# A gated FFT-filter and feed-forward kernel: x and part of w1 loaded first, the gate moved to VectorE and GpSimd, w2 moved to SyncE's queue, and the scheduler's transfer rates reset

## The chip, the cores and the metric

The kernel runs on one core of one Trainium2 chip. The time is device microseconds (us) of one execution. Each quoted time is a median of several fast executions. An execution counts as slow when it is over 1.5% above the fastest of the same kernel. "Span" is the length of the one profiled execution, from its first to its last instruction; it is about 2 us shorter than the time of that execution.

## The reference

```python
B, S, D, F = 1, 2048, 512, 1792              # x: (1, 2048, 512), bfloat16
g = sigmoid((x * gate_w).sum(-1, keepdims=True))
a = irfft2(rfft2(x) * (w_r + 1j * w_i))      # over (S, D)
h = x @ w1 + b1                              # (S, F)
b = (h * tanh(softplus(h))) @ w2             # Mish, then (S, D)
out = g * a + (1 - g) * b
```

Two independent paths read x, and the gate g joins them at the very end. TensorE does the Fourier transforms as matrix products. Two transposes between the stages go through scratch in device memory ("scr" in the profile).

## The kernel before

x is taken in 16 tiles of 128 rows. All work is declared as tasks with reads, writes and a priority. When the kernel is built, a list scheduler inside it gives each engine a fixed order of its tasks. It does this with its own guesses of how long everything takes. On the chip every engine goes through its list in order. When the head of the list isn't ready, the engine waits, even if later items could run.

```python
SYNC_LAT = 0.12
DMA_BW = 370e3        # bytes per us that the scheduler assumes for a transfer
XBAR_BW = 95e3
W_BW = 150e3          # ... for the reversed loads of w_r, w_i
NEARLY = 12           # tiles whose feed-forward result is parked before the last stage
# priorities: the ready task with the highest one goes first
PR = dict(ld=100.0, tr=99.5, a1=98.0, s1=99.0, mid=96.0, fin=94.0, mm1=80.0,
          act=90.0, mm2=70.0, out=95.0, gate=99.8, cp=95.5)
# ... in schedule(), for each task taken:
            free[t.eng] = est + t.dur
            if t.isdma:
                xs = max(est + t.dur + 1.2, bw_free)
                bw_free = xs + t.xfer          # t.xfer = bytes / bw
                t.done = bw_free + 0.9
            else:
                t.done = est + t.dur
            order[t.eng].append(t)
```

The five stages of TensorE work, under the names used below:

- **First stage**: FFT along D and part of S, 16 tiles. Its result is written to scratch and read back transposed.
- **Middle stage**: the rest of the FFT along S, the multiplication by w (on VectorE) and the first inverse step, 16 pairs; then scratch again.
- **Last stage**: the remaining inverse steps, then the mixing with g on VectorE.
- **First product**: x @ w1, 224 matmuls of 512 columns (after Mish on ScalarE, its result feeds the next).
- **Second product**: the Mish result @ w2, another 224 matmuls' worth.

The two products depend on the FFT nowhere. They are the *filler* that the scheduler puts into TensorE's list wherever it thinks that the FFT will not be ready. The second product can fill only once w2 has landed.

```python
        # loads, in order of issue on SyncE's queue (SP)
        ld_x(0, 1)
        ld_c(0, 0, 1280, ["FD", ("FT", 0)])    # FFT tables
        ld_x(1, 4)
        ld_w1(0)                               # first half of w1
        ld_c(1, 1280, 2816, [("FT", 1)])
        ld_x(4, 8)
        ld_w1(1)
        # ... rest of x, w_r, w_i, then:
        for o, W in (("Wa", Wa), ("Wb", Wb)):  # copy to the other half of the partitions
            for h in range(2):
                # ...
                G.add(f"cp{o}{h}", [("dve", ..., lambda e, ...: e.tensor_scalar(
                    out=W[64:128, js, :], in0=W[0:64, js, :], scalar1=sc, ...))],
                      reads=[(o, i) for i in range(4)], writes=[(o, 4, h)], prio=PR["cp"])
        # ... t_r1w: the four writes of the first stage's result to scratch
        for h in range(2):                     # w2 on GpSimd's queue, behind those writes
            dma(f"ld_w2_{h}", w2_sb[:, 7*h:7*(h+1), :], w2v[:, 7*h:7*(h+1), :], 128 * 7 * 1024,
                writes=[("w2", h)], deps=t_r1w, queue="pool")
        # ... the first product reads w1 in halves (ft // 7):
        G.add(f"mm1_{c}_{ft}", ..., reads=[...] + [("w1", ft // 7)], ..., prio=PR["mm1"] - 3 * c)
        # ... second product:
        G.add(f"mm2_{t}_{part}_{n0}", ..., prio=PR["mm2"] - 6 * c - 0.01 * n0)

        # the gate: 64 one-column matmuls, Tanh on ScalarE after all Mish, then the columns
        def f_gate(e):
            for t in range(NT):
                for dt_ in range(4):
                    ins = e.matmul(ps[:, bk(sl_g), t:t + 1], xT[:, dt_, t, :],
                                   gw_sb[:, dt_:dt_ + 1], start=(dt_ == 0), stop=(dt_ == 3))
            return ins
        G.add("gate", ..., deps=t_hs[-2:-1], prio=PR["gate"])
        G.add("gth", [("act", 1.6, lambda e: e.activation(gth[:, :], ps[:, bk(sl_g), 0:NT],
              AF.Tanh, scale=0.5))], reads=[sl_g], writes=["gth"], deps=t_hs, prio=PR["gate"])
        # gcol = 0.5 * gth + 0.5, omg = 0.5 - 0.5 * gth, ngcol = -gcol   (VectorE)
```

## Time and profile before

| before | |
|---|---|
| time, median of 3 runs | 146.09 us (145.66 to 146.83) |
| span of the profiled run | 142.7 us |
| TensorE busy | 134.9 us, 95% |
| first product starts | 9.86 us |
| first middle-stage matmul | 42.05 us |
| gate columns start on VectorE | 99.00 us |

The page of the profile gives busy time by engine, then each engine's busy tenths in 40 equal slices (9 is 90% or more), the granted clock and the DMA engines in the same slices, and shares of the chain of waits that ended last. PE is TensorE, DVE VectorE, ACT ScalarE, POOL GpSimd, SP SyncE. Lines of the page of the kernel before:

```profile
span 142.7 us, 2376 instructions
...
PE 134.9 (95%) x866; PEld 72.9 (51%) x881; DVE 86.1 (60%) x188; ACT 82.9 (58%) x139; POOL 3.9 (3%) x10
...
PE   6999999778979999999999999999999999999992
...
DMA  4999999999299999580303695000012120100121
...
PE 70%; DVE 13%; DMA 7%; ACT 4%; issue 3%; DVEq 0%; SPq 0%
```

TensorE is the limit: 95% busy, and most of the chain. The only slices below 9 between the first and the last are 8, 9, 10 and 12, which lie between about 25 and 43 us. The view of waits, for TensorE alone, says for what it stood (line waiting, what ended the wait, us in total, times, the longest):

```profile
PE ps L666 <- DVE R L515: 1.5, 2, 0.8
PE ps L530 <- DVE GD L527: 1.3, 1, 1.3
PE ps L748 <- DMA R<-scr: 0.8, 1, 0.8
PE ps L703 <- ACT hsb L812: 0.5, 1, 0.5
PE ps L824 <- DMA w_sb<-in_B_w_dram: 0.2, 1, 0.2
```

An eviction is the copy of a TensorE result out of PSUM, the memory that matmuls write to; VectorE does it as a CAST, ScalarE as an ACTIVATE. L666 is the first stage, L748 the first middle-stage matmul, L703 a small table step, L824 the second product, and L530 the warm-up at the start. The timeline lists start, duration, engine, line, operation, count, and in brackets the idle time before and what ended it. These lines of the kernel before (of several engines) show the two waits on VectorE, the wait for scratch, and the gate:

```profile
25.09 1.23 DVE L583 TENSOR_SCALAR Wa<-Wa 64x4112 bf16<-64x4112 bf16 x1 [1.94 <-DMA Wa<-in_A_w_r_dram]
...
26.34 1.29 DVE L515 CAST R<-ps 128x512 bf16<-128x512 f32 x2
...
27.09 0.28 PE L666 MATMUL ps<-CF,R 128*128 128x256 bf16 x1 [0.78 <-DVE R L515]
...
42.05 0.28 PE L748 MATMUL ps<-R,SM 128*128 128x256 bf16 x1 [0.76 <-DMA R<-scr]
...
95.64 1.74 PE L845 MATMUL ps<-gw_sb,xT 128*128 128x1 bf16 x64
...
97.49 1.28 ACT L849 ACT_TABLE_LOAD   x1 [2.47 <-PE ps L845]
...
99.00 0.17 DVE L852 TENSOR_SCALAR gcol<-gth 128x16 f32<-128x16 f32 x1 [12.28 <-ACT gth L849]
```

The first-stage matmul at 27.09 needs an eviction (CAST) that stood in VectorE's list behind a 1.23 us copy of Wa. The gate's 64 matmuls take 1.74 us, counted until the last result is out; then come a table load, Tanh and the column arithmetic. The Trainium skill, "ScalarE: Activation LUTs", section "What ACT_TABLE_LOAD costs", states about 1283 ns for such a load; the trace's 1.28 us agrees.

### The profile page before, as it was taken

The page shows a single profiled execution, that of the slowest core. Times are in us where ns is not written, and L with a number is a line of the kernel's source. Part 1 is how long each engine was busy: PE and PEld are TensorE (multiplying, and loading weights), DVE is VectorE, ACT ScalarE, POOL GpSimd, SP SyncE. Part 2 cuts the span into 40 slices and gives each one's busy share as a digit, 9 for nine tenths or more (in the row PEclk, how much of TensorE's full clock was granted, in tenths as well). Part 3 has the DMA queues.
Part 4 walks back from the last instruction along what each step waited for, and adds up shares of the span by engine and source line. Part 5 has one row for each costly group of instructions (what it writes and reads, how often), then busy time and mean ns, then how long its engine had stood idle before and what let it go on. Part 6 is the DMA issues. An engine that isn't in the chain of part 4 may idle for free.

```text
span 142.7 us, 2376 instructions
## 1 busy us (share of the span) xinstructions
PE 134.9 (95%) x866; PEld 72.9 (51%) x881; DVE 86.1 (60%) x188; ACT 82.9 (58%) x139; POOL 3.9 (3%) x10
## 2 busy tenths in 40 slices
PE   6999999778979999999999999999999999999992
PEld 2476665554434444434444465455456565555471
DVE  2448694974009999999971031002999985899331
ACT  3289888776867877779984573855154344431000
POOL 1000000000160000000000000000000000000000
PEclk9999999999999999999999999999999999999999
DMA  4999999999299999580303695000012120100121
GB/s 117 302 405 408 249 172 151 150 307 336 74 310 359 364 317 145 131 283 0 147 0 152 174 292 121 0 0 5 0 74 76 74 76 5 74 0 36 43 108 39
DMA packets 20463, 21.66 MB, mean 152 GB/s; under 512 B 5156, under 2 KB 16932, under 8 KB 20388
## 3 DMA queue, kind: packets, MB, share of 16 engines
q1 hardware_dynamic: 19712, 18.89, 49.6%
q0 software_dynamic: 704, 2.62, 5.2%
q8 instruction: 7, 0.11, 0.3%
q14 instruction: 4, 0.03, 0.1%
q10 hardware_dynamic: 36, 0.00, 0.0%
HBM read 14.17 MB, written 6.29 MB: 143 GB/s over the span
## 4 chain that ended last, share of the span: by engine, by line
PE 70%; DVE 13%; DMA 7%; ACT 4%; issue 3%; DVEq 0%; SPq 0%
PE ps L824 28%; PE ps L804 21%; PE ps L885 5%; PE ps L530 4%; DMA scr<-R 4%; DVE PX L764 3%; DVE PX L760 3%; DVE PX L763 3%; DMA R<-scr 3%; PE ps L866 3%; PE ps L654 2%; ACT R L516 2%; DVE PX L767 2%; DVE R L515 1%; PE ps L779 1%
## 5 line engine op out<-in xcount | busy, mean ns | idle before, releaser
L824 PE MATMUL ps<-w_sb,hsb 128*128 128x512 bf16 (+1 forms) x232 | 51.3, 366 | 0.6 <-DMA w_sb<-in_B_w_dram 0.2
L804 PE MATMUL ps<-xT,w_sb 128*128 128x512 bf16 x215 | 51.3, 379 | 0.4
L812 ACT ACTIVATE hsb<-ps,b1f 128x512 bf16<-128x512 f32 x56 | 37.7, 689 | 11.1 <-PE ps L804 10.8
L516 ACT ACTIVATE R<-ps 128x512 bf16<-128x512 f32 (+1 forms) x43 | 24.7, 596 | 16.3 <-PE ps L824 11.2
L824 PEld LDWEIGHTS ps<-w_sb,hsb 128*128 128x128 bf16 x238 | 22.7, 98 | 22.4 <-DMA w_sb<-in_B_w_dram 0.5
L804 PEld LDWEIGHTS ps<-xT,w_sb 128*128 128x128 bf16 x224 | 21.2, 98 | 22.9 <-ACT xT L621 0.2
L516 ACT ACTIVATE PX<-ps 128x512 bf16<-128x512 f32 (+1 forms) x19 | 10.5, 551 | 6.8 <-PE ps L885 4.2
L515 DVE CAST R<-ps 128x512 bf16<-128x512 f32 (+1 forms) x17 | 11.3, 689 | 3.3 <-PE ps L654 1.6
L876 ACT ACTIVATE TT<-ps 128x512 bf16<-128x512 f32 x11 | 6.4, 595 | 6.5 <-PE ps L866 6.4
L897 DVE SCALAR_TENSOR_TENSOR PX<-ps,gcol,R 128x512 f32<-128x512 f32 x12 | 9.0, 751 | 1.4 <-DVE R L891 0.5
L873 DVE CAST TT<-ps 128x512 bf16<-128x512 f32 x5 | 3.4, 689 | 9.7 <-PE ps L866 8.9
L885 PE MATMUL ps<-GD,TT 128*128 128x256 bf16 x64 | 9.0, 273 | 0.0
L530 PE MATMUL ps<-GD 128*128 128x512 bf16 x18 | 7.3, 522 | 1.3 <-DVE GD L527 1.3
L885 PEld LDWEIGHTS ps<-GD,TT 128*128 128x128 bf16 x64 | 6.2, 98 | 3.3 <-DVE TT L873 0.3
L852 DVE TENSOR_SCALAR gcol<-gth 128x16 f32<-128x16 f32 x1 | 0.2, 174 | 12.3 <-ACT gth L849 12.3
L767 DVE TENSOR_TENSOR PX<-PX 128x512 bf16<-128x512 bf16 x16 | 6.8, 425 | 1.0
L763 DVE TENSOR_TENSOR PX<-PX,Wb 64x512 bf16<-64x512 bf16 x16 | 6.8, 422 | 0.5
L764 DVE TENSOR_TENSOR PX<-PX,Wb 64x512 bf16<-64x512 bf16 x16 | 6.7, 421 | 0.2
L760 DVE TENSOR_TENSOR PX<-PX,Wa 128x512 bf16<-128x512 bf16 x16 | 6.7, 421 | 0.1
L923 DVE SCALAR_TENSOR_TENSOR R<-ps,omg,R 128x512 bf16<-128x512 f32 (+1 forms) x5 | 3.2, 643 | 5.8 <-PE ps L824 5.8
L903 DVE SCALAR_TENSOR_TENSOR R<-ps,gcol,PX 128x256 bf16<-128x256 f32 x12 | 5.8, 484 | 0.4
L654 PEld LDWEIGHTS ps<-CF,R 128*128 128x128 bf16 x64 | 4.7, 101 | 2.6 <-issue 0.6
(93 smaller groups left out, 110.9 us busy)
## 6 DMA issues: line engine op xcount, KB each, us to landing
scr<-R SPq DMA_DIRECT2D x8, 512.0 KB, 4.6
R<-scr SPq DMA_DIRECT2D x8, 512.0 KB, 6.0
w_sb<-in_B_w_dram SPq DMA_DIRECT2D x2, 896.0 KB, 8.8
w_sb<-in_B_w_dram POOLq DMA_DIRECT2D x2, 896.0 KB, 11.4
out_dram<-R SPq DMA_DIRECT2D x7, 256.0 KB, 2.0
R<-in_A_x_dram SPq DMA_DIRECT2D x3, 512.0 KB, 11.3
SM<-c_sm SPq DMA_DIRECT2D x1, 576.0 KB, 10.9
Wa<-in_A_w_r_dram SPq DMA_DIRECT2D x1, 514.0 KB, 13.9
```

The costliest lines, as they stand in the source:

```text
L515: G.add(name, [("dve", dve_dur(n), lambda e: e.tensor_copy(out=outf(), in_=inf())), ("act", act_dur(n), lambda e: e.activation(outf(), inf ...
L516: ("act", act_dur(n), lambda e: e.activation(outf(), inf(), AF.Copy))],
L530: G.add(f"warm{i}", [("pe", 0.43 if i < 7 else 0.22, lambda e, sl=sl: e.matmul(ps[:, bk(sl), :], GDf[:, 0:128], GDf[:, 0:512], start=True, ...
L760: return e.tensor_tensor(out=v(P1, sP, 0, 128), in0=v(Xb, sX, 0, 128), in1=Wa[:, js, 0:256], op=ALU.mult)
L763: e.tensor_tensor(out=v(P2, sQ, 0, 64), in0=v(Xb, sX, 64, 128), in1=Wb[64:128, js, 0:256], op=ALU.mult)
L764: return e.tensor_tensor(out=v(P2, sQ, 64, 128), in0=v(Xb, sX, 0, 64), in1=Wb[0:64, js, 0:256], op=ALU.mult)
L767: return e.tensor_tensor(out=P1[:, sP.i, :], in0=P1[:, sP.i, :], in1=P2[:, sQ.i, :], op=ALU.add)
L804: ins = e.matmul(ps[:, bk(sl), :], w1_sb[:, dt_, 128 * ft:128 * (ft + 1)], xT[:, dt_, 4 * c:4 * c + 4, :], start=(dt_ == 0), stop=(dt_ == 3))
L812: return e.activation(hsb[:, hb, ft, :], ps[:, bk(sl), :], AF.Mish, bias=b1f[:, ft:ft + 1])
L824: ins = e.matmul(ps[:, bk(sl), 0:n1 - n0], hsb[:, hb, ft, 128 * tl:128 * (tl + 1)], w2_sb[:, ft, n0:n1], start=(ft == 0), stop=(ft == NFT ...
L885: ins = e.matmul(ps[:, bk(sy), 256 * hh:256 * (hh + 1)], TT[:, st.i, i, :], GD[:, i, :], start=(i % 2 == 0), stop=(i % 2 == 1))
L897: return e.scalar_tensor_tensor(out=o, in0=ps[:, bk(sy), 0:256].unsqueeze(1).to_broadcast([128, 2, 256]), scalar=gcol[:, t:t + 1], in1=ya[ ...
```

## The change

The intent: let TensorE start real work earlier, give it more filler while the first scratch round trip is under way (so w2 has to be there earlier), and take the gate off TensorE and ScalarE, where it sits between the products and the last stage.

The diff, cut to its core:

```diff
-NEARLY = 12
+NEARLY = 8
-DMA_BW = 370e3
+DMA_BW = 380e3
-W_BW = 150e3
+W_BW = 130e3
 # (and given rates at single transfers: scratch writes 330e3 and 300e3, scratch reads
 #  300e3 and 296e3, the straight part of w_r, w_i 188e3, first x tiles 600e3 and 270e3)

 # start
-        ld_x(0, 1)
-        ld_c(0, 0, 1280, ...)
-        ld_x(1, 4)
-        ld_w1(0)                                  # half of w1
+        ld_x(0, 1, bw=600e3)
+        ld_x(1, 4, bw=270e3)
+        ld_w1(0)                                  # 512 of its 1792 columns
+        ld_c(0, 0, 1280, ...)
+        ld_w1(1)

 # w2
-        for h in range(2):
-            dma(f"ld_w2_{h}", ..., deps=t_r1w, queue="pool")
-        dma("ld_gd", ..., deps=t_r1w, queue="pool")          # inverse tables
-        dma("ld_gt", ..., deps=t_s1 + t_r1w, queue="pool")
+        ld_w2(0)                  # on SyncE's queue, right behind w_r, w_i and SM (middle-stage tables)
+        ld_w2(1, t_e2)            # t_e2: the evictions of the first stage
+        dma("ld_gd", ..., deps=t_e2)
+        dma("ld_gt", ..., deps=t_s1 + t_r1r)                 # t_r1r: the scratch reads

 # copies of Wa, Wb
-                      reads=[(o, i) for i in range(4)], writes=[(o, 4, h)], prio=PR["cp"])
+                      reads=[(o, i) for i in range(4)], writes=[(o, 4, h)], deps=t_e2, prio=PR["cp"])

 # second product
-    prio=PR["mm2"] - 6 * c - 0.01 * n0
+    prio=(76.0, 75.0, 58.0, 52.0)[c] - 0.01 * n0

 # gate
-        G.add("gate", 64 matmuls ...); G.add("gth", Tanh on ScalarE ...)
+        for h in range(4):
+            dma(f"ld_xg{h}", xg[:, 4*h:4*h+4, :], xv[:, 4*h:4*h+4, :], 128 * 4096, ...)  # x again
+            for t in range(4 * h, 4 * h + 4):
+                G.add(f"gx{t}", [("dve", 0.8, lambda e, t=t: e.scalar_tensor_tensor(
+                    out=xg[:, t, :], in0=xg[:, t, :], scalar=1.0, in1=gwb[:, :],
+                    op0=ALU.mult, op1=ALU.mult, accum_out=gacc[:, t:t + 1]))], ...)
+        # z = clip(gacc, -80, 80); ez = e ** z by GpSimd pow; omg = 1 / (1 + ez); gcol = ez * omg
```

There is also a rewrite of how the late tiles of the last stage are mixed, which goes with NEARLY = 8: the gate scale is applied on the way out of PSUM instead of in a separate step. Some small priorities and the scheduler's guess for the warm-up matmuls change too. The rates are used nowhere but in the scheduler. They transfer nothing faster; they only change what it believes, and so its order.

## The prediction

> **What bounds the kernel now.** TensorE: the page has it busy 95% of 142.7 us, 70% of the chain of waits; the stretch table shows granted clock 1.00. In the chain a 512-column matmul takes 0.216 us back to back. By counts: the feed-forward products 448 x 0.216 = 96.7; FFT first stage 8.9, middle 6.9, inverse 10.6; transposes 1.8; gate 1.6: about 126.5 us. The other 16.2 (stretches, timeline): start 7.2 (warm-up matmuls, waiting for x and w1); two late warm-ups 0.4; idle between 12 and 140 us 3.9; tail 2.5; 2.2 unassigned. Stalls (waits): 0.78 and 0.75 at 26.3 and 28.9 us (waiting for an eviction behind a 1.23 us copy of Wa on VectorE); 0.46 at 33.9 (table step); 0.76 at 42.0 (scratch read); 0.25 at 51.8 (w2).
>
> **What the change does.**
> 1. Gate off TensorE: 64 one-column matmuls, 1.58 us at 95.8, on the chain: saved. The Tanh table load (1.28 us at 97.5) goes too, off the path; the Trainium skill, "ScalarE: Activation LUTs", "What ACT_TABLE_LOAD costs", has 1283 ns; the trace agrees. The 16 new VectorE multiply-accumulates, 0.65 us each (estimate from the 0.64 us scalar-tensor-tensor), 10.4 us, fit VectorE's idle 76 to 97 us. GpSimd pow: no duration to go by.
> 2. Wa/Wb copies moved behind all evictions: the two 0.75 us stalls go (-1.5).
> 3. More fill: 112 first-product and 14 second-product matmuls stand ahead of the first middle matmul, against 88. Scratch, table and w2 stalls go (-1.4).
> 4. x, then 512 KB of w1, then tables: first product at about 7.8 instead of 9.9 us, no warm-up afterwards: -0.7.
> 5. DMA runs full from 4 to 36 us; w2's first half and the broadcast gate add 1.0 MB ahead of the scratch writes, 3 us at the trace's 340 GB/s, so scratch reads land at 44 to 48 instead of 42 us; the fill hides it. The Trainium skill, "DMA: Bandwidth & Descriptors", "Issuing engines are not separate DMA queues", has all issuers share 16 engines: w2 on SP gains only by starting earlier, into the 36 to 40 us gap (DMA 0.34 busy).
> 6. Given back: in the middle stage the filler is 7 matmuls per pair (1.94 us with the FFT's two) instead of 8 (2.16), while VectorE needs about 2.0: it becomes the limit, +1.5. The stage runs 47 to 79 us, not 42 to 75.
> 7. Late-tile rewrite (8 early tiles, not 12): VectorE 29 us against 35 us of TensorE work in the last stage; off the path.
>
> Sum: -1.6 -1.5 -1.4 -0.7 -0.4 (small) +1.5 = -4.1 if the middle loses in full, about -6 if not; I take -5.3.
>
> **Predicted: 140.8 us, 8 in 10 within 138.8 to 143.3.** Faster by over 2%: 0.87; within 2%: 0.11; slower: 0.02.
>
> **What would show it right:** no gate matmuls or second table load late; no waits over 0.5 us of first-stage matmuls on VectorE; first middle matmul at 46 to 49 us; VectorE over 95% busy in the middle stage with TensorE at 92 to 97%; gate columns ready before the chain needs them. **Wrong:** TensorE waiting on w2's second half or scratch reads near 44 to 48 us.
>
> **What would make it wrong.** w2's second half and inverse tables queue ahead of the scratch reads and stall the middle stage by several us; the second x load delays the second scratch round trip; pow takes over 6 us; the first w1 part lands after 8 us.

## The result, and the profile after

| | before | after |
|---|---|---|
| time, median (fast runs, same rounds) | 145.88 us (4 runs, 144.66 to 146.83) | 139.32 us (4 runs, 138.44 to 139.75) |
| ratio | | 0.957, 95% interval 0.9485 to 0.9655 |
| span | 142.7 us | 136.6 us |
| TensorE busy | 134.9 us, 95% | 131.3 us, 96% |
| VectorE busy | 86.1 us, 60% | 94.1 us, 69% |
| first product starts | 9.86 us | 7.76 us |
| first middle-stage matmul | 42.05 us | 45.40 us |
| 512-column feed-forward matmuls listed ahead of it | 88 | 126 (112 + 14) |

A ratio is the mean time of one kernel's fast runs over that of the other's of the same rounds, so it isn't quite the ratio of the quoted medians. The counts in the last row are read from the instruction order of the built kernels, not from the trace, which lacks some matmul records. In a pair such as 112 + 14, the first number is of the first product, the second of the second.

The page of the kernel after:

```profile
span 136.6 us, 2281 instructions
...
PE 131.3 (96%) x803; PEld 70.6 (52%) x817; DVE 94.1 (69%) x213; ACT 82.4 (60%) x137; POOL 3.6 (3%) x8
...
PE   6999999999999999999999999999999999999992
...
DMA  4999999999999923658853535990002101222021
...
PE 77%; DVE 17%; issue 4%; DVEq 0%
```

TensorE has no slice below 9 between the first and the last, and DMA is gone from the chain. TensorE's waits in the kernel after, all of them:

```profile
PE ps L537 <- DVE GD L534: 1.2, 1, 1.2
PE ps L783 <- DVE PX L771: 0.3, 1, 0.3
PE ps L816 <- issue: 0.2, 1, 0.2
```

Only the wait at the start is left, with two small ones (L783 is the inverse step of the middle stage). Its timeline around the scratch read and around the gate (the lines are of several engines and not adjacent):

```profile
42.38 3.19 PE L836 MATMUL ps<-w_sb,hsb 128*128 128x512 bf16 x14
45.40 0.27 PE L752 MATMUL ps<-R,SM 128*128 128x256 bf16 x1
...
77.42 0.68 DVE L802 SCALAR_TENSOR_TENSOR R<-R,gwb 128x512 bf16<-128x512 bf16 x1
...
95.78 2.91 POOL L856 TENSOR_TENSOR gz<-eul,gz 128x16 f32<-128x16 f32 x1 [94.37 <-DVE gz L855]
...
99.22 0.17 DVE L859 TENSOR_TENSOR gcol<-gz,omg 128x16 f32<-128x16 f32 x1
...
101.08 0.47 DVE L909 SCALAR_TENSOR_TENSOR R<-ps,ngcol,PX 128x256 bf16<-128x256 f32 x1
...
101.71 0.39 PE L871 MATMUL ps<-CF,R 128*128 128x128 bf16 x4
```

Fourteen second-product matmuls run up to the first middle-stage matmul, which has no idle time in front of it. They can only be there because w2's first half has landed. At the gate, VectorE gets the last quarter of the second load of x at 92.85 us; pow then takes 2.91 us on GpSimd while TensorE goes on with the first product. VectorE finishes the first tile of the last stage at 101.55 (101.08 + 0.47), and TensorE's next last-stage matmuls follow at 101.71. So the gate delays nothing, but at its end there is only about 0.15 us to spare.

**Where the 6.1 us of span went**, divided at the first middle-stage matmul. In the kernel after it starts 3.35 us later (45.40 against 42.05), but 38 more feed-forward matmuls of 0.216 us are done by then, 8.2 us of work: 4.9 us are won ahead of this point. From there to the end it takes 91.2 us against 100.65, 9.45 us less, for 9.8 us less work (the 8.2 and the gate's 1.6). So the gate's 1.6 us are won and about 0.35 us given back: 4.9 + 1.6 - 0.35 is the 6.1.

### The profile page after: what moved, and what is told of

Read it like the earlier page. It is cut to its first block, busy times and chain, and to the rows that moved or that the text cites. A ratio compares the mean times of both kernels' runs of the same rounds, so it can differ in the third digit from the quotient of the medians.

```text
span 136.6 us, 2281 instructions
## 1 busy us (share of the span) xinstructions
PE 131.3 (96%) x803; PEld 70.6 (52%) x817; DVE 94.1 (69%) x213; ACT 82.4 (60%) x137; POOL 3.6 (3%) x8
## 4 chain that ended last, share of the span: by engine, by line
PE 77%; DVE 17%; issue 4%; DVEq 0%
PE ps L816 35%; PE ps L836 21%; PE ps L890 5%; PE ps L537 4%; DVE PX L768 4%; DVE PX L767 4%; DVE PX L764 4%; DVE PX L771 3%; PE ps L652 3%; PE ps L871 3%; PE ps L610 1%; PE ps L664 1%; PE ps L665 1%; DVE R L518 1%; PE ps L783 1%
## 5 line engine op out<-in xcount | busy, mean ns | idle before, releaser
L816 PE MATMUL ps<-xT,w_sb 128*128 128x512 bf16 x216 | 49.7, 379 | 0.6 <-issue 0.2
L519 ACT ACTIVATE R<-ps 128x512 bf16<-128x512 f32 (+1 forms) x37 | 20.9, 596 | 8.1 <-PE ps L836 4.1
L518 DVE CAST R<-ps 128x512 bf16<-128x512 f32 (+1 forms) x19 | 12.7, 689 | 5.5 <-PE ps L652 3.8
L519 ACT ACTIVATE PX<-ps 128x512 bf16<-128x512 f32 x15 | 8.9, 597 | 5.8 <-DVE PX L764 2.2
L802 DVE SCALAR_TENSOR_TENSOR R<-R,gwb 128x512 bf16<-128x512 bf16 x16 | 10.0, 688 | 1.1 <-DMA R<-in_A_x_dram 1.1
L927 DVE SCALAR_TENSOR_TENSOR R<-ps,omg,R 128x512 bf16<-128x512 f32 (+1 forms) x9 | 6.2, 692 | 5.9 <-PE ps L836 5.7
L914 ACT ACTIVATE PX<-ps,gcol 128x256 f32<-128x256 f32 x8 | 3.7, 473 | 6.9 <-PE ps L890 6.9
L537 PE MATMUL ps<-GD 128*128 128x512 bf16 x18 | 6.0, 475 | 1.2 <-DVE GD L534 1.2
L902 DVE SCALAR_TENSOR_TENSOR PX<-ps,gcol,R 128x512 f32<-128x512 f32 x8 | 6.0, 752 | 0.7
L783 PE MATMUL ps<-PX,SM 128*128 128x512 bf16 x15 | 5.7, 381 | 0.4 <-DVE PX L771 0.3
## 6 DMA issues: line engine op xcount, KB each, us to landing
w_sb<-in_B_w_dram SPq DMA_DIRECT2D x2, 896.0 KB, 10.7
```

Of the source, the lines that this page charges most:

```text
L518: t = G.add(name, [("dve", dve_dur(n), lambda e: e.tensor_copy(out=outf(), in_=inf())), ("act", act_dur(n), lambda e: e.activation(outf(), ...
L519: ("act", act_dur(n), lambda e: e.activation(outf(), inf(), AF.Copy))],
L537: G.add(f"warm{i}", [("pe", 0.42 if i < 5 else 0.22, lambda e, sl=sl: e.matmul(ps[:, bk(sl), :], GDf[:, 0:128], GDf[:, 0:512], start=True, ...
L802: G.add(f"gx{t}", [("dve", 0.8, lambda e, t=t: e.scalar_tensor_tensor(out=xg[:, t, :], in0=xg[:, t, :], scalar=1.0, in1=gwb[:, :], op0=ALU ...
L816: ins = e.matmul(ps[:, bk(sl), :], w1_sb[:, dt_, 128 * ft:128 * (ft + 1)], xT[:, dt_, 4 * c:4 * c + 4, :], start=(dt_ == 0), stop=(dt_ == 3))
```

## The experiments

Two readings of that division compete.

- **The ledger**, on which the prediction was built: each part removes its own stall or work, and the parts add up.
- **The order**: what counts is whether the scheduler's fixed list has the right amount of filler at each point where the FFT depends on something slow. Then a part has no worth of its own. It may even cost, because it moves the list.

All twelve runs gave correct results and were timed in five rounds. "Ratio" is to the kernel before, which ran in the same rounds (medians 144.74, 144.85 and 144.88 us in the three groups); brackets are the 95% interval. Line numbers differ a little from kernel to kernel. Where the granted clock was below 1.00 for a while, this is said.

### Group 1: the kernel after, and one part of it undone

**after_again**: the kernel after, unedited.

> The changed kernel once more, as the yardstick for the runs beside it. All theories: ratio to before about 0.957 (0.950 to 0.963), profiled span 136.5 to 138, TensorE idle after 12 us about 1.5 us in sum.

Ratio 0.9592 [0.9559, 0.9625], median 138.87 us, span 136.9 us. The result repeats, on another set of rounds and with a narrower interval.

**a_gate_on_tensor**: the gate goes back to TensorE and ScalarE; the second load of x, the broadcast gate weights and pow go out.

```diff
-        for h in range(4): dma(f"ld_xg{h}", ...); 16 multiply-accumulates on VectorE; pow ...
+        G.add("gate", [("pe", 64 * 0.03, f_gate)], ..., deps=t_hs[-2:-1], prio=PR["gate"])
+        G.add("gth", [("act", 1.6, ... AF.Tanh ...)], ..., deps=t_hs, prio=PR["gate"])
```

> The changed kernel with the old gate: 64 one-column matmuls, Tanh on ScalarE, no second x load, no pow. Ledger theory (only TensorE time counts): 1.6 us slower than the changed kernel, ratio about 0.968, the 64 matmuls on the chain for 1.6 us and no other new TensorE wait above 0.5 us. Rival 1 (the gain is the latency of the gate: VectorE's 12 us wait and the late start of the last stage): 3 us or more slower, ratio 0.978 or above, with TensorE waiting in the last stage. Rival 2 (the gain is the order of the loads): unchanged or faster, ratio 0.957 or below, for 2 MB less is loaded.

Ratio 0.9908 [0.988, 0.9937], median 143.52 us, span 141.3 us. That is 4.65 us over after_again, for matmuls that take 1.6. The timeline shows the other three:

```profile
103.73 1.74 PE L851 MATMUL ps<-gw_sb,xT 128*128 128x1 bf16 x64
...
105.34 6.20 PE L830 MATMUL ps<-w_sb,hsb 128*128 128x512 bf16 x28
...
107.09 0.17 DVE L858 TENSOR_SCALAR gcol<-gth 128x16 f32<-128x16 f32 x1 [14.87 <-ACT gth L855]
...
111.38 0.39 PE L872 MATMUL ps<-CF,R 128*128 128x128 bf16 x4
```

And from its view of waits:

```profile
PE ps L891 <- ACT TT L882: 1.5, 2, 0.8
```

Tanh is put after all Mish, and so after the whole first product. In this order the first product runs until 102.4 us, against 94.3 in the kernel before, so the gate's columns come at 107.09 instead of 99.00. TensorE spends 28 second-product matmuls, 6.2 us, on covering the wait. These are then missing as filler between the last-stage tiles, and TensorE waits there twice for ScalarE (1.5 us) and runs at the pace of VectorE, which mixes one tile in about 2 us (the gate-scaled steps start at 107.76, 109.79 and 111.81). In sum TensorE is busy 2.3 us longer than in after_again (134.9 against 132.6) and waits 2.0 us longer (3.5 against 1.5), which is nearly the whole difference of the spans, 4.4. The gate's position is worth more than its duration. Of the readings, this fits Rival 1; b_gate_off_tensor below shows that an earlier gate alone brings nothing in the kernel before.

**a_copies_early**: the copies of Wa and Wb are no longer held back.

```diff
-                      ..., writes=[(o, 4, h)], deps=t_e2, prio=PR["cp"])
+                      ..., writes=[(o, 4, h)], prio=PR["cp"])
```

> The changed kernel with the Wa/Wb copies no longer held behind the last first-stage eviction. The scheduler reorders the FFT matmuls a little around them. Ledger theory: TensorE waits of 0.5 us or more on evictions come back near 25 to 31 us, 0.7 to 1.5 us in sum, ratio about 0.964. Rivals 1 and 2: no change, 0.957.

Ratio 0.9605 [0.9574, 0.9636], median 139.12 us: 0.25 us over after_again, with overlapping intervals. The copies are back between the evictions, at 25.61 and 28.19 us on VectorE, much as in the kernel before, and yet TensorE has no wait on an eviction. All its waits:

```profile
PE ps L537 <- DVE GD L534: 1.2, 1, 1.2
PE ps L783 <- DVE PX L771: 0.3, 1, 0.3
```

The list has four first-product matmuls between the first-stage tiles there, which cover it. So the two waits of 0.75 us in the kernel before came from the copies together with an order that had nothing to put in front of them.

**a_w2_gpsimd**: w2 and the inverse tables go back to GpSimd's queue, behind the scratch writes.

```diff
-        ld_w2(0)
-        ld_w2(1, t_e2)
+        ld_w2(0, t_r1w)                    # with queue="pool" inside ld_w2
+        ld_w2(1, t_r1w)
-        dma("ld_gd", ..., deps=t_e2)
+        dma("ld_gd", ..., deps=t_r1w, queue="pool")        # and ld_gt likewise
```

> The changed kernel with both halves of w2 and both inverse tables on the GpSimd queue behind the scratch writes, as before. By the instruction order the 14 second-product matmuls ahead of the middle stage are then gone, and 112 first-product ones remain. Ledger theory: scratch reads land earlier (42 to 43 us), so the lost filler costs only a short wait there plus waits for w2 at 44 to 52 us: 0.3 to 1.5 us slower, ratio 0.959 to 0.967. Rival 2: at least 3 us slower, 0.978 or above. Rival 1: no change.

Ratio 1.0172 [1.0138, 1.0207], median 147.4 us: 8.5 us over after_again, slower than the kernel before. One line of the timeline matters most:

```profile
49.82 3.17 PE L836 MATMUL ps<-w_sb,hsb 128*128 128x512 bf16 x7 [5.10 <-DMA w_sb<-in_B_w_dram]
```

TensorE came to the second product before w2 was there and waited 5.1 us. The wait itself had a price: seven matmuls took 3.17 us instead of the 1.67 that seven take elsewhere, because the granted clock had dropped to 0.50. It was half from about 48.2 to 55.0 us, so it had fallen while TensorE was still waiting.

### Group 2: the kernel before, with one part of the change alone

**b_gate_off_tensor**: the new gate, with its loads and pow.

```diff
-        G.add("gate", 64 matmuls ...); G.add("gth", Tanh ...)
+        (second load of x, 16 multiply-accumulates, pow, columns, as in the change)
```

> The kernel before with the new gate alone (VectorE products from a second x load, pow on GpSimd, no Tanh). Undoing it cost the changed kernel 4.6 us where the ledger had 1.6, so two readings are open. Ledger: 1.6 us faster than before, ratio 0.989. Coupled reading (the late gate also forces second-product matmuls, which are filler, to be spent ahead of the last stage, and there TensorE then waits for VectorE): in the kernel before, whose first-product matmuls end at 95 us anyway and whose last stage shows no TensorE wait, the extra part is absent, so also 1.6 (0.986 to 0.991); a larger gain, 3 us or more (0.979 or below), would say that the latency of the gate counts by itself.

Ratio 1.0006 [0.9954, 1.0059], median 144.72 us. The gate's 1.6 us on TensorE are gone, and the whole has gained nothing. In the view of waits the first-stage wait on evictions went from 1.5 to 2.2 us, scratch from 0.8 to 1.0, and waits of 0.6 (on the Wb copy), 0.5 and 0.5 us (last stage, on VectorE) and 0.4 us (w2) stand in their place.

**b_copies_late**: the copies wait for the evictions of the first stage.

```diff
-                      ..., writes=[(o, 4, h)], prio=PR["cp"])
+                      ..., writes=[(o, 4, h)], deps=t_e2, prio=PR["cp"])
```

> The kernel before with the Wa/Wb copies moved behind the last first-stage eviction, nothing else. Ledger: the two TensorE waits of 0.75 us at 26 and 29 us go, 1.5 us faster, ratio about 0.990. If they only turn into a wait for the scratch read a few us later (the scratch writes are held by the queue, not by the evictions), the ratio is 0.997 to 1.003.

Ratio 1.0133 [1.0079, 1.0188], median 146.62 us: slower. The two waits on evictions are gone, as meant. But the first stage now ends earlier with only 84 filler matmuls on the list ahead of the scratch read, and the whole gain and more goes into one wait:

```profile
41.31 0.40 PE L749 MATMUL ps<-R,SM 128*128 128x256 bf16 x1 [3.44 <-DMA R<-scr]
...
42.99 4.76 PE L805 MATMUL ps<-xT,w_sb 128*128 128x512 bf16 x12
```

Again the clock fell after the wait. Lines from the stretch table of the same run (stretch, its length; then TensorE, weight loads, VectorE, ScalarE and GpSimd busy with counts; then the granted clock, DMA share, GB/s):

```profile
40.00:41.00 1.00, 0.00 (x0) 0.00 (x0) 0.00 (x0) 0.00 (x0) 0.91 (x2) 0.61 0.96 348
...
44.00:45.00 1.00, 1.00 (x4) 0.30 (x3) 0.86 (x3) 0.05 (x1) 0.00 (x0) 0.50 1.00 406
...
48.00:49.00 1.00, 1.00 (x6) 0.49 (x5) 0.87 (x3) 0.99 (x2) 0.00 (x0) 1.00 1.03 352
```

TensorE is "busy" 1.00 in the last two; at half clock it begins 4 matmuls in a microsecond, at full clock 6. The half clock lasted from about 40.2 to 47.0 us: the first line, with no matmul in it, already has a mean of 0.61.

**b_w2_hardware**: w2 and the inverse tables on SyncE's queue, placed as in the change.

```diff
-            dma(f"ld_w2_{h}", ..., deps=t_r1w, queue="pool")
+        ld_w2(0)                    # behind SM
+        ld_w2(1, t_e2)              # GD after t_e2, GT after the scratch reads
```

> The kernel before with w2 and the inverse tables on the SyncE queue as in the change, nothing else. The queue reading (the gain is w2 on the hardware queue): 3 us or more faster, 0.98 or below. Coupled reading: the kernel before still had first-product matmuls to fill with until w2 came and waited 0.25 us for it; w2 first puts 0.9 MB ahead of the scratch writes, the scratch reads land near 45 us instead of 42, and the start leaves too little fill: no gain or a loss of up to 2 us, ratio 0.997 to 1.014.

Ratio 1.0222 [1.0172, 1.0272], median 147.97 us: slower, by 1.7 to 2.7%. The extra bytes ahead of the scratch reads delay them, and the list, with 100 filler matmuls, doesn't reach:

```profile
46.61 0.28 PE L750 MATMUL ps<-R,SM 128*128 128x256 bf16 x1 [2.41 <-DMA R<-scr]
```

Waits of 2.3 us on evictions and 0.8 and 0.7 us in the first product come on top. The scratch reads are issued at 42.16 us, against 37.97 in the kernel before. (The profiled execution, 149.02 us, is the slowest of the six.) The other queue and the earlier place buy nothing by themselves. The Trainium skill, "DMA: Bandwidth & Descriptors", section "Issuing engines are not separate DMA queues", says that transfers started by any engine run on the same 16 DMA engines, and that issuing from several saves only sequencer time. The traces fit this, though no run changes the queue and leaves the place: a half of w2 takes 11.4 us from issue to landing on GpSimd's queue in the kernel before, and 10.7 us on SyncE's in the kernel after.

**b_new_start**: the new order of the first loads, with the scheduler's rates for them.

```diff
-        ld_x(0, 1); ld_c(0, ...); ld_x(1, 4); ld_w1(0); ld_c(1, ...); ld_x(4, 8); ld_w1(1)
+        ld_x(0, 1, bw=600e3); ld_x(1, 4, bw=270e3); ld_w1(0); ld_c(0, ...); ld_w1(1); ld_x(4, 8); ld_c(1, ...)
```

> The kernel before with the new order of the first loads (x, 512 KB of w1, tables) and its modelled rates, nothing else. Ledger: first product at 7.8 instead of 9.9 us, 0.7 us faster, ratio 0.995. Coupled reading: the time won is lost again at the scratch read or at w2, since both come no earlier: 0.997 to 1.003, with TensorE waits near 42 or 48 us that grow by as much as the start wins.

Ratio 0.9995 [0.995, 1.0039], median 144.67 us: nothing. One of the two waits on evictions is gone (0.7 us in place of 1.5), but TensorE waits 2.1 us for w2 and 1.3 us for ScalarE at the table step, where the kernel before has 0.2 and 0.5:

```profile
PE ps L824 <- DMA w_sb<-in_B_w_dram: 2.1, 2, 1.7
PE ps L703 <- ACT hsb L812: 1.3, 1, 1.3
```

The earlier start makes TensorE arrive earlier at the next thing that isn't there.

By the ledger each of these four parts should have gained or at least cost nothing. Measured they are 1.0006, 1.0133, 1.0222 and 0.9995. If they multiplied, the product would be 1.036, and the change gives 0.959. The ledger falls here. What none of these runs contains is the set of rates for scratch, w_r and w_i, which looked like a detail (nor do they contain the late-tile rewrite and the new priorities, of which the last run below is free too).

### Group 3: the order alone

**a_old_rates**: the kernel after with the scheduler's rates of before (those of the first x and w1 loads are left as in the change).

```diff
-DMA_BW = 380e3
+DMA_BW = 370e3
-W_BW = 130e3
+W_BW = 150e3
 # and the single rates of the scratch transfers and of w_r, w_i removed
```

> The changed kernel with the old transfer rates in the kernel's own scheduler (370 and 150 in place of 380 and 130, and none of the special rates); the same operations on the same data, only their order on the engines differs. Order theory (the gain needs an instruction order that fits when the scratch data really land): 108 feed-forward matmuls stand ahead of the first middle matmul instead of 126, so TensorE comes to it near 42 us and waits about 3 us for the scratch read, and may lose its clock after that: 3 to 6 us slower than the changed kernel, ratio 0.98 to 1.00. Operations theory (each operation moved or removed is worth its own TensorE time): unchanged, 0.957 to 0.963.

Ratio 1.0031 [0.9975, 1.0088], median 145.97 us, span 143.3 us. The whole gain is gone, and this kernel differs from the one after in no task and in no byte moved. Only the order differs (and with it which of VectorE and ScalarE takes an eviction: VectorE has 216 instructions instead of 213). The list has 108 + 0 matmuls ahead of the first middle-stage one instead of 112 + 14. Two of TensorE's lines:

```profile
45.02 0.28 PE L752 MATMUL ps<-R,SM 128*128 128x256 bf16 x1 [2.75 <-DMA R<-scr]
...
102.99 0.38 PE L871 MATMUL ps<-CF,R 128*128 128x128 bf16 x4 [2.54 <-DVE R L909]
```

And three of the gate's:

```profile
94.12 0.69 DVE L802 SCALAR_TENSOR_TENSOR R<-R,gwb 128x512 bf16<-128x512 bf16 x1 [2.97 <-DMA R<-in_A_x_dram]
...
97.06 2.92 POOL L856 TENSOR_TENSOR gz<-eul,gz 128x16 f32<-128x16 f32 x1 [95.64 <-DVE gz L855]
...
100.51 0.17 DVE L859 TENSOR_TENSOR gcol<-gz,omg 128x16 f32<-128x16 f32 x1
```

The data is there at about 45.0 us, and TensorE had come to this point of its list 2.75 us before. In the kernel after it comes there at 45.40, with the fourteen second-product matmuls done, and doesn't wait. The second line is the gate: VectorE waits for the last quarter of x until 94.12, the columns come late, and TensorE loses 2.54 us there. All this is at full clock in the profiled execution. In four of the six executions (one of them slow, and left out) the mean granted clock was 0.977 to 0.988, so part of the median is lost clock; but the two executions at 0.999 and 1.000 (144.45 and 145.09 us) are still 5.6 and 6.2 us above after_again.

**b_new_rates**: the rates alone, on the kernel before.

```diff
-DMA_BW = 370e3
+DMA_BW = 380e3
-W_BW = 150e3
+W_BW = 130e3
 # and the single rates of the scratch transfers and of w_r, w_i as in the change
```

> The kernel before with only the new transfer rates in its scheduler; again the same operations in another order. 104 instead of 88 matmuls ahead of the first middle matmul, so the wait of 0.8 us for the scratch read goes; but second-product matmuls are now placed from about 46 us, and w2 by the GpSimd queue landed only at about 51 us. Order theory: a TensorE wait for w2 of 2 us or more, ratio 1.00 to 1.03: right rates alone give nothing without an early w2. If the new order alone were the gain: 0.97 or below.

Ratio 1.0392 [1.0338, 1.0446], median 150.96 us: the worst of all. The wait for scratch is gone, as these rates were meant to do. But the order now brings the second product early, and w2 still arrives late on GpSimd's queue:

```profile
50.28 3.17 PE L824 MATMUL ps<-w_sb,hsb 128*128 128x512 bf16 x7 [4.40 <-DMA w_sb<-in_B_w_dram]
```

4.4 us of waiting, then half clock until about 55.7 us. Waits of 1.9 and 1.4 us on VectorE and 1.0 us on ScalarE come on top.

**b_w2_rates**: the kernel before, with the edits of b_w2_hardware and of b_new_rates together.

```diff
+ (edit of b_w2_hardware)
+ (edit of b_new_rates)
```

> The kernel before with w2 on the SyncE queue (alone: 1.022) and the new rates together; old gate, old start, copies not held back. 119 matmuls ahead of the first middle matmul. Order theory: the two together gain where each alone does not: no wait above 0.5 us at the scratch read or for w2, ratio 0.975 to 0.995. Operations theory: the sum of the two alone, above 1.0.

Ratio 0.9811 [0.9746, 0.9875], median 142.21 us. Two edits that cost 2.2% and 3.9% alone gain 1.9% together. 112 + 7 matmuls stand ahead of the first middle-stage one, and TensorE waits neither for scratch nor for w2. Its waits on evictions (0.9 and 0.4 us) and on ScalarE (0.5 us) remain, and so does the gate.

**b_gate_w2_start_rates**: the same, with the edits of b_gate_off_tensor and b_new_start too. What it lacks of the change is the held-back copies, the rewrite of the late tiles with NEARLY = 8, the new priorities of the second product and one small priority at the table step.

```diff
+ (edits of b_w2_rates, b_gate_off_tensor and b_new_start)
```

> The kernel before with new gate, w2 on SyncE, new start and new rates; without the held-back copies, the 8 early tiles with their rewritten last steps, and the new priorities of the second product. Order theory: these left-out parts matter little (undoing the copies cost 0.1%), so ratio 0.957 to 0.967, the whole gain. If the rewritten last steps or the priorities carry a share: 0.97 or above.

Ratio 0.9596 [0.9551, 0.9641], median 139.29 us, span 137.7 us. This is the whole gain (0.9592 in group 1). The list has 112 + 14 matmuls ahead, as in the kernel after, and the waits are those of the kernel after but for 0.4 us in the last stage:

```profile
PE ps L535 <- DVE GD L532: 1.2, 1, 1.2
PE ps L867 <- DVE R L905: 0.4, 1, 0.4
PE ps L780 <- DVE PX L768: 0.3, 1, 0.3
PE ps L812 <- issue: 0.2, 1, 0.2
```

The runs side by side (filler is the number of 512-column feed-forward matmuls listed ahead of the first middle-stage matmul; waits are TensorE's, in us):

| kernel | filler | scratch wait | w2 wait | ratio |
|---|---|---|---|---|
| before | 88 | 0.8 | 0.2 | 1 |
| b_copies_late | 84 | 3.4 | none | 1.0133 |
| b_new_start | 96 | none | 2.1 | 0.9995 |
| b_w2_hardware | 100 | 2.4 | none | 1.0222 |
| b_new_rates | 104 | none | 4.4 | 1.0392 |
| a_old_rates | 108 | 2.7 | none | 1.0031 |
| a_w2_gpsimd | 112 + 0 | none | 5.1 | 1.0172 |
| b_w2_rates | 112 + 7 | none | none | 0.9811 |
| a_gate_on_tensor | 112 + 14 | none | none | 0.9908 |
| b_gate_w2_start_rates | 112 + 14 | none | none | 0.9596 |
| after_again | 112 + 14 | none | none | 0.9592 |

The filler count alone doesn't decide, because the scratch read lands at another time in each. What does is whether the list is long enough for when the data lands, and whether what is on the list has landed itself. Only kernels with w2 early *and* the new rates have neither wait, and only those that also have the gate off TensorE and ScalarE reach 0.96.

**What the scheduler believed.** The kernels were built once more with the scheduler's own times printed; these are its plan, not measurements. In the kernels with 112 + 14 the first middle-stage matmul starts within 0.7 us of the plan (kernel after: planned 46.1, in the trace 45.4). In all the others but one it starts 1.2 to 5.6 us later than planned (a_old_rates: 42.3 and 45.0), by a wait for scratch or by stalls before it. The exception is a_w2_gpsimd (43.2 and 43.7), where w2 is what comes late: planned for 45.5 us, it is waited for until 49.8. This speaks for the order reading: in the kernels that gain in full, the plan comes true. The gate shows the same: a_old_rates plans its columns (gcol) for 94.3 us and has them at 100.7, the kernel after plans 99.5 and has them at 99.4. The latter is partly luck. In both, the scheduler takes pow for 0.4 us where it needs 2.9; in the kernel after this is made up for by other wrong guesses, such as 0.8 us for each multiply-accumulate that takes 0.61.

**Expectations missed.** The readings often had the direction and not the size. b_gate_off_tensor and b_copies_late fell outside every range named. b_w2_hardware, b_new_rates and a_old_rates went the way that the order reading said, but further: 1.0222 against at most 1.014, 1.0392 against at most 1.03, and 7.1 us against 3 to 6. The ledger's figure was missed in every run that named one, in b_new_start only just.

**The clock after a wait.** In the traces with waits of 3.44, 4.40 and 5.10 us (b_copies_late, b_new_rates, a_w2_gpsimd) the granted clock fell to 0.50 while TensorE still waited, 2.35, 3.00 and 3.48 us after its last matmul, and stayed there for 6.83 us each time. In the traces with waits of 2.41 and 2.75 us (b_w2_hardware, a_old_rates) it did not fall. The Trainium skill, "TensorE: Matmul & The Clock Gate", section "What's actually happening", says that after an idle window of about 3.4 us the array falls to half its clock. That only the longer waits lost it fits this, but the 2.35 us does not: the clock can fall sooner, and no run here shows a threshold. Nor does a kernel lose the same each time: the mean granted clock of the six executions of b_copies_late lies between 0.976 and 0.988, and in a_old_rates four of six lost some. In the three traces the half clock lasted 5.7, 5.4 and 5.2 us from the restart, so each of these waits cost another 2.6 to 2.9 us (half of that time, as an estimate).

## Why the prediction was right or wrong

The time was right: 140.8 us predicted, with 138.8 to 143.3 as the range; measured 139.32. The reason given for it, a sum of independent terms, was wrong as a sum of the parts' own worths, though the division of the trace comes close to it (4.0 us predicted ahead of the middle stage, 1.6 for the gate, against 4.9 and 1.6). It comes close because the prediction took its stalls and its filler (126 against 88) from the whole change as built, where the waits did go; what it had wrong is which part removes them.

1. **Gate off TensorE, -1.6.** Right for the kernel after, where 1.6 us less work is on TensorE. Wrong as what this part is worth: taken alone it is worth nothing (1.0006), and taken out of the changed kernel it costs 4.65 us. What the step left out is that Tanh had to wait for all Mish, so that the old gate forbids running the first product late. The table load was said to be off the path. In the kernel before that holds; in a_gate_on_tensor it lies in the wait for the gate's columns. The estimate of 0.65 us for each multiply-accumulate was close: 0.61 us from start to start, 0.69 with its end.
2. **Copies held back, -1.5.** This term failed. Both waits are gone in the kernel after, but undoing this part brings none of them back and changes the time by 0.25 us, within the intervals. Done alone it costs 1.3%. Either the move or the order removes the two waits; in the changed kernel the order is enough.
3. **More fill, -1.4.** The mechanism is right and is the core of the change: no wait for scratch, table step or w2 is left. Two things were missed. The fill doesn't come with w2's earlier load alone: it takes the rates in the scheduler as well (a_old_rates has every other part and 2.7 us of scratch wait; b_new_rates has the rates without w2 and waits 4.4 us for it). And its size was only the waits that can be seen, whereas a wrong order costs much more than it had cost so far: up to 5.1 us of wait with a halved clock behind it.
4. **Earlier start, -0.7.** First product at 7.76 us, predicted 7.8. Alone it gains nothing (0.9995).
5. **Scratch reads later but hidden.** The first middle-stage matmul came at 45.40 us, a little earlier than the 46 to 49 predicted, with no wait. The named danger (w2 in front of the scratch reads) is real: b_w2_hardware shows it, with 2.4 us. It is the new rates that make the list long enough (a_old_rates).
6. **Middle stage gives back up to 1.5.** Over-sized in full. The prediction's test was VectorE over 95% busy and TensorE at 92 to 97%; in the stretch from 54 to 80 us of the kernel after VectorE has 24.41 of 26 us (94%) and TensorE 25.59 (98%):

```profile
54.00:80.00 26.00, 25.59 (x115) 11.31 (x119) 24.41 (x63) 18.07 (x32) 0.00 (x0) 1.00 0.56 167
```

   VectorE is nearly the limit there, but not quite. By the division above, about 0.35 us were given back behind the first middle-stage matmul. The point estimate had taken only about 0.3 of the 1.5, so that this cost it little; nothing in the prediction singles out this share, so the fit is luck.
7. **Rewrite of the late tiles off the path.** b_gate_w2_start_rates is without it and has the whole gain; this agrees.

The gate columns were to be ready before the chain needs them. They were, with about 0.15 us to spare, which is far less than "pow takes over 6 us" as a danger supposed: at 2.91 us it already was nearly on the path, behind the second load of x. No run made pow longer, so this rests on the timeline.

Where the span was 0.8 us better than the sum (6.1 against the 5.3 taken), the difference is in the front part (4.9 against 4.0). Some of it is probably in the waits themselves: a lone matmul of 512 columns is shown as busy for 0.38 us, in a row each takes 0.216, so behind each wait some 0.16 us of drain (the last results on their way out) count as busy. For the five waits that went or shrank this makes about 0.8 us, an estimate that no run tests.

What stays open: no run changed the number of filler matmuls alone, or w2's queue without its place; how the gain divides among w2, rates, gate and start can't be stated, since their worth depends on what else is there; the interplay of the new start with the rest was not run by itself; and whether a shorter warm-up, which the profile leaves as the largest remaining wait at the start, would gain anything was not run. No kernel was clearly faster than the changed one.

## What to carry to other kernels

In a kernel whose order is fixed when it is built, ask of each slow dependency how much independent work the list has ahead of it, and whether that work's own inputs are there. A part that removes a wait can be worth nothing or less until its partners are in (2.2% and 3.9% lost alone, 1.9% won together), so test combinations and re-tune the scheduler's constants with every move of a load. Don't price an operation by its duration alone: its place in the order decided here between 0 and 4.65 us for 1.6 us of matmuls; and look at the granted clock behind every wait of some 2.5 us or more (here the waits of 3.4 us and more had half a clock behind them). Compare the scheduler's plan with the trace: where they part, look for the wait.

## What the Trainium skill lacked or had wrong

- "GPSIMD Engine Reference" has no duration for pow. A tensor-tensor pow of 128x16 float32 took 2.91 to 2.94 us here, which lay almost on the path.
- "VectorE: DVE Perf Modes" has no duration for a scalar-tensor-tensor. With accumulator, 128x512 bfloat16 took 0.69 us (0.61 from start to start) with both inputs in SBUF, followed by an accumulator read of 0.08 us; the section "Two Vector instructions with no wait between them" does say that such an operation is two instructions, and the trace agrees.
- "TensorE: Matmul & The Clock Gate" gives about 3.4 us of sustained work for the return to full clock, in a free-running window. After three long waits it took 5.2, 5.4 and 5.7 us from the restart of the matmuls. For the fall it gives an idle window of about 3.4 us; here it came 2.35, 3.00 and 3.48 us after the last matmul. In each case the half clock lasted 6.83 us, of which only the part after the restart cost time.
- No page speaks of a scheduler's assumed transfer rates as something to be tuned with a change; the same tasks in another order were 139 or 146 us (after_again, a_old_rates).
